# A spectral filter and an MLP on one core: the MLP's second step with weights held and tokens run past

## The chip, the cores and the metric

One core of one Trainium2 chip runs the whole program. The metric is the device time of one execution in microseconds (us). The kernel before took 2520.49 us (median of three runs, 2520.19 to 2525.57). Engines: TensorE (PE, its weight loads PEld), VectorE (DVE), ScalarE (ACT), GpSimd (POOL) and SyncE (SP), which here only issues DMAs.

## What is computed

```python
B, S, D, DFF = 8, 3008, 256, 2048
X = np.fft.rfft(x, axis=1)                       # x: 8 x 3008 x 256
y = np.fft.irfft(X * (filt_r + 1j * filt_i), n=S, axis=1)
t = y.reshape(B * S, D)                          # 24064 tokens
h = t @ w_in                                     # 256 -> 2048
g = h / (1 + np.exp(-1.702 * h))
out = g @ w_out                                  # 2048 -> 256, float32
```

## The kernel before, in words

The sequence length is 64 x 47, so each transform is two matrix steps with a trip through DRAM between them. `fft(b)` does the forward transform, the filter product and the first inverse step of batch b in 46 pieces (`yield`s); `signal(b, t)` does the last inverse step for one tile of tokens and leaves the tile `y` with features on the partitions and tokens along the row, split into a high and a low float32r part. `mlp(b, t, y, nb)` then runs the MLP on a tile of nb blocks of 128 tokens: 4 blocks (512 tokens) in 44 of the 48 tiles, 3 blocks in the last tile of the even batches.

All products of the MLP are done three times, high x high, high x low and low x high, and summed in PSUM. The hidden width is cut into NFC = 16 chunks of 128. `first(fc)` (L592 to L604) does chunk fc of the first step: six matmuls with a 128x128 piece of `wi` held and 512 tokens run past, into a PSUM tile `h`; ACT reads it twice (L601 into `g`, L602 rounded into `gh`) and DVE takes the rest (L603, `gl`). `second(fc)` (L606 to L615) adds chunk fc to the output: for each of the four blocks, the block's `gh` is held and the 512 columns of `wo` (256 high, 256 low) run past (L611), then its `gl` is held and the 256 high columns run past (L615). Each block has a PSUM bank of its own, `pos[i]`, with tokens on partitions. After the last chunk, ACT and DVE add the two halves of each bank into `out` (L625, L626), and SP stores whole rows of 1 KB: two DMAs for a tile (L632), and two of one row per partition (L634) in the four tiles that also carry a row of the neighbouring batch.

PSUM has 8 banks: 2 in the pool `ps_f` (everything of the transforms and of `signal`), 2 in `ps_h` (the chunks `h`), 4 in `ps_o` (`pos`). In the very first transform, `bank` takes tiles from all three pools in turn (L249).

The main loop (L662) goes through the tiles; between the chunks of tile i it lets the next batch's transform take its pieces and, after two of the chunks, the next tile's `signal`. Each engine runs its own instructions in a fixed order; the framework's scheduler chooses that order from an estimated timeline, so it need not be that of the source. The weights arrive as 64-bit floats; `weight` (L184) turns them into float32 and splits them into high (ACT, L209) and low (POOL, L210) parts during tile 0. `wo` lies as [128, chunk, high/low, 256].

Of the kernel before, what the change touches and what calls it, by code (L numbers as in the profile page):

```python
# [9 lines left out]
F32 = mybir.dt.float32  # L10
F32R = mybir.dt.float32r
# [3 lines left out]
ALU = mybir.AluOpType  # L15

B, S, D, DFF = 8, 3008, 256, 2048
N1, N2 = 64, 47
NS = 32
NH = 24  # L20
P = 128
Q = 112
NFC = DFF // P
# [79 lines left out]
def tile_kernel(  # L103
# [12 lines left out]
    nc = tc.nc  # L116
    const = ctx.enter_context(tc.tile_pool(name="const", bufs=1))
    sb = ctx.enter_context(tc.tile_pool(name="sb", bufs=2))
    dram = ctx.enter_context(tc.tile_pool(name="dram", bufs=2, space=bass.MemoryType.DRAM))
    dram1 = ctx.enter_context(tc.tile_pool(name="dram1", bufs=1, space=bass.MemoryType.DRAM))  # L120
    ps_f = ctx.enter_context(tc.tile_pool(name="ps_f", bufs=2, space=bass.MemoryType.PSUM))
    ps_h = ctx.enter_context(tc.tile_pool(name="ps_h", bufs=2, space=bass.MemoryType.PSUM))
    ps_o = ctx.enter_context(tc.tile_pool(name="ps_o", bufs=4, space=bass.MemoryType.PSUM))

    def raw(name):
        return sb.tile([P, 4, D], F32, tag="raw", name=name, bufs=6)
# [16 lines left out]
    HALF = NFC // 2  # L143
    wi_sb, wo_sb = [], []
# [9 lines left out]
    def down(v, q, n=4):  # L154

        return v[:, NH - 1 - q : (NH - 1 - n - q if q + n < NH else None) : -1, :]
# [24 lines left out]
        load_in(w, src)  # L181
        return w

    def weight(w, tu):  # L184

        if w.dtype != F32:
            rv = w.bitcast(U32).rearrange("p a (n k) -> p a n k", k=2)
            low, top = rv[:, :, :, 0], rv[:, :, :, 1]
            t, u = (a.bitcast(U32) for a in tu)
            w = t.bitcast(F32)  # L190


            ins = nc.scalar.activation(t.bitcast(F32), top.bitcast(F32), AF.Abs)
            if first[0]:
                tc.keep_in_program_order(ins)
                first[0] -= 1
            hi, lo = yield
            nc.vector.tensor_scalar(t.bitcast(F32), t.bitcast(F32), LEAST, MOST, ALU.max, ALU.min)
            nc.vector.tensor_scalar(u, t, 3, 0x40000000, ALU.logical_shift_left, ALU.bitwise_xor)
            nc.vector.tensor_scalar(t, u, 0xFF800000, None, ALU.bitwise_and)  # L200
            nc.vector.scalar_tensor_tensor(w, low, 2.0**-52, t.bitcast(F32), ALU.mult, ALU.mult)  # L201
            nc.gpsimd.tensor_tensor(w, u.bitcast(F32), w, ALU.add)
            nc.scalar.activation(w, w, AF.Abs)
            nc.vector.scalar_tensor_tensor(
                w.bitcast(U32), top, 0x80000000, w.bitcast(U32), ALU.bitwise_and, ALU.bitwise_or
            )
        else:
            hi, lo = yield
        nc.scalar.copy(hi, w)  # L209
        nc.gpsimd.tensor_tensor(lo, w, hi.bitcast(F32), ALU.subtract)  # L210
        yield

    def weights():

        todo, tus = [], None
        for i in range(NFC + 4):
            if i < NFC:
                c = slice(P * (i - i % 2), P * (i - i % 2) + 2 * P)
                src = w_out[c, :].rearrange("(c p) d -> p c d", p=P) if i % 2 else w_in[:, c].rearrange("(k p) c -> p k c", p=P)
                todo.append(load_weight(src, f"w_{i}"))  # L220
            if i >= 4:
                if tus is None:
                    tus = const.tile([P, 4, 2, 2, D], F32, tag="zy", name="w_tu")
                for k in range(4 if i == 4 else 1):
                    k = k if i == 4 else i - 1
                    if k < NFC:
                        todo[k] = weight(todo[k], [tus[:, k % 4, m] for m in range(2)])
                        next(todo[k])
                n, o = divmod(i - 4, HALF)
                if n == len(wi_sb):  # L230
                    wi_sb.append(const.tile([P, 2, 2, DFF // 2], F32R, tag=f"wi_{n}", name=f"wi_{n}"))
                    wo_sb.append(const.tile([P, HALF, 2, D], F32R, tag=f"wo_{n}", name=f"wo_{n}"))
                if i % 2:
                    to = [wo_sb[n][:, o - 1 : o + 1, k, :] for k in range(2)]
                else:
                    to = [wi_sb[n][:, k, :, P * o : P * o + 2 * P] for k in range(2)]
                todo[i - 4].send(to)
            yield

    b_of = {}  # L240

    zy = []

# [2 lines left out]
        nc.tensor.matmul(ps, wh, ml, start=False, stop=False)  # L246
        nc.tensor.matmul(ps, wl, mh, start=False, stop=True)  # L247

    banks = [(ps_f, "f"), (ps_o, "o"), (ps_h, "h"), (ps_o, "o")]  # L249
    n_bank = [0]  # L250

    def bank(name):
# [332 lines left out]

    def mlp(b, t, y, nb):

        w = P * nb
        pos = [ps_o.tile([P, 2, D], F32, tag="o", name=f"o_{b}_{t}_{i}") for i in range(nb)]
        gs = {}  # L590

        def first(fc):  # L592
            ps = ps_h.tile([P, 512], F32, tag="h", name=f"h_{b}_{t}_{fc}")
            half, o = divmod(fc, HALF)
            c = slice(P * o, P * o + P)
            for n, (kc, wk, yk) in enumerate([(k, *q) for k in range(2) for q in ((0, 0), (0, 1), (1, 0))]):
                nc.tensor.matmul(ps[:, :w], wi_sb[half][:, wk, kc, c], y[:, yk, kc, :w], start=n == 0, stop=n == 5)  # L597
            g = sb.tile([P, 512], F32, tag="g", name=f"g_{b}_{t}_{fc}")
            gh = sb.tile([P, 512], F32R, tag="gh", name=f"gh_{b}_{t}_{fc}")
            gl = sb.tile([P, 512], F32R, tag="gl", name=f"gl_{b}_{t}_{fc}")  # L600
            nc.scalar.activation(g[:, :w], ps[:, :w], AF.Gelu_apprx_sigmoid)  # L601
            nc.scalar.activation(gh[:, :w], ps[:, :w], AF.Gelu_apprx_sigmoid)  # L602
            nc.vector.tensor_tensor(gl[:, :w], g[:, :w], gh[:, :w].bitcast(F32), ALU.subtract)  # L603
            gs[fc] = gh, gl  # L604

        def second(fc):  # L606
            gh, gl = gs.pop(fc)
            wo = wo_sb[fc // HALF][:, fc % HALF]
            for i in range(nb):
                c = slice(P * i, P * i + P)  # L610
                nc.tensor.matmul(  # L611
                    pos[i].rearrange("p k d -> p (k d)"), gh[:, c],
                    wo.rearrange("p k d -> p (k d)"), start=fc == 0, stop=False,
                )
                nc.tensor.matmul(pos[i][:, 0, :], gl[:, c], wo[:, 0, :], start=False, stop=fc == NFC - 1)  # L615

        first(0)
        for fc in range(NFC):
            if fc + 1 < NFC:
                first(fc + 1)  # L620
            second(fc)
            yield
        o = sb.tile([P, 4, D], F32, tag="out", name=f"out_{b}_{t}")
        for i in range(nb):
            nc.scalar.copy(o[:, i, :], pos[i][:, 1, :])  # L625
            nc.vector.tensor_tensor(o[:, i, :], pos[i][:, 0, :], o[:, i, :], ALU.add)  # L626
        full = 4 if t < 5 else 3
        ov = out.rearrange("(b a n) d -> b a n d", b=B, n=N2)
        for j in range(2):
            n = NH * j + 4 * t  # L630
            dst = ov[b, :, n : n + full, :] if j else down(ov[b], 4 * t)[:, 0:full]
            nc.sync.dma_start(dst, o[64 * j : 64 * j + 64, 0:full, :])  # L632
            if nb > full:
                nc.sync.dma_start(ov[b - 1 + j, :, 0, :], o[64 * j : 64 * j + 64, 3, :])  # L634

    def run(gen, n=None):
        while n is None or n > 0:
# [24 lines left out]
    for i, (b, t) in enumerate(tiles):  # L662
        if t == 0:

            done, chunk, chunks = 0, 0, 6 * NFC - (18 if b == 0 else 8)
            nxt = fft(b + 1) if b + 1 < B else iter(())
        nb = 4 if t < 5 or b % 2 else 3
        sig = start(*tiles[i + 1]) if i + 1 < len(tiles) else iter(())
        for fc, _ in enumerate(mlp(b, t, ys.pop((b, t)), nb)):
            if i == 0:  # L670
                run(w_parts, 1)
                if fc < 5:
                    qs = slice(4 * fc + 4, 4 * fc + 8)
                    load_in(t2_sb[:, qs], t2[:, qs])
                if fc == 12:
                    split_de(de_of[0])
                    tc.keep_in_program_order(nc.vector.memset(f_buf[32:64], 0.0))
                    load_filter()
                    in_order[0] = False
            if i or fc >= 10:  # L680
                chunk += 1
                while chunk <= chunks and done < STEPS * chunk // chunks:
                    run(nxt, 1)
                    done += 1
            if fc in ((11, 13) if t == 5 else (3, 9)):
                run(sig, 1)
        run(sig)
        if i == 0:
            zy.append(const.tile([P, 4, 2, 2, D], F32R, tag="zy", name="zy"))
            nc.gpsimd.memset(zy[0][32:64].bitcast(F32), 0.0)  # L690


_OUTS = [((B * S, D), "float32")]
# [22 lines left out]
```

## Time and profile before

| what | value |
|---|---|
| median of three runs | 2520.49 us |
| profiled execution | 2525.12 us |
| its span, first to last instruction | 2523.3 us |
| granted TensorE clock, mean over the span | 0.987 |
| PE / PEld busy | 96% / 81% |
| DVE / ACT / POOL busy | 62% / 53% / 34% |
| HBM read / written | 158.15 MB / 100.14 MB |

A matmul's record is longer than the slot it takes, since the next one starts while it drains; so the pace of PE is read from the starts of consecutive instructions and not from their durations. In a timeline, consecutive instructions of one kind on an engine are merged into one row with their count. A share of busy time is an average over stages with different limits.

### The profile page before, as it was taken

To read this page: it belongs to the slowest core of one execution; us is meant where nothing else is said; L and a number is where in the kernel's file an instruction comes from. 1 tells how busy PE (TensorE), PEld (TensorE's weight loads), DVE (VectorE), ACT (ScalarE), POOL (GpSimd) and SP (SyncE) were. 2 spreads that over 40 slices of the span, in tenths; PEclk is the share of its full clock that TensorE was granted. 3 is DMA by queue.
4 is the path that set the end of the run, shared out by engine and by line. 5 is a ranking of instruction groups with operands and counts; after the bars stand their busy time and mean duration, and the time that the engine had idled before them with its cause. 6 is when DMAs were issued, how large, how long until landed. Compare 5 with 4: busy or idle time off the path is not lost.

```text
span 2523.3 us, 35230 instructions
## 1 busy us (share of the span) xinstructions
PE 2433.0 (96%) x12540; PEld 2053.8 (81%) x12540; DVE 1556.5 (62%) x2309; ACT 1349.6 (53%) x2546; POOL 847.6 (34%) x734
## 2 busy tenths in 40 slices
PE   5679998999999999999999999999999999999998
PEld 3368887888888888888888888888888888888887
DVE  5784887367763777547773577646775377742222
ACT  4455555555555555555555555555555555644443
POOL 4462443234332444224441344324342244410000
PEclk8789999999999999999999999999999999999999
DMA  8757343453435433453434444355343543330000
GB/s 200 191 153 178 88 97 94 119 126 87 93 92 142 101 92 92 124 132 84 107 80 124 120 102 97 95 130 115 91 100 92 139 95 91 91 71 9 17 9 17
DMA packets 183227, 257.53 MB, mean 102 GB/s; under 512 B 18560, under 2 KB 132910, under 8 KB 183052
## 3 DMA queue, kind: packets, MB, share of 16 engines
q1 hardware_dynamic: 100492, 140.04, 22.0%
q10 hardware_dynamic: 57056, 70.80, 10.5%
q0 software_dynamic: 25504, 44.44, 9.0%
q8 instruction: 100, 1.64, 0.3%
q14 instruction: 75, 0.61, 0.1%
HBM read 158.15 MB, written 100.14 MB: 102 GB/s over the span
## 4 chain that ended last, share of the span: by engine, by line
PE 87%; DMA 5%; DVE 3%; issue 2%; ACT 1%; SPq 0%; POOL 0%; ACTq 0%; DVEq 0%; POOLq 0%
PE h L597 38%; PE o L611 26%; PE o L615 13%; PE i L572 3%; PE s L507 2%; PE i L507 2%; DMA zy<-a_d 1%; DMA br<-b_d 1%; DMA x<-in_x_dram 1%; PE s L245 1%; PE s L247 1%; PE s L246 1%; DVE gl L603 1%; DMA b_d<-b 1%; SPq L135 0%
## 5 line engine op out<-in xcount | busy, mean ns | idle before, releaser
L597 PE MATMUL h<-y,wi 128*128 128x512 f32 (+1 forms) x4608 | 1182.4, 388 | 8.6 <-ACT wi L209 6.8
L603 DVE TENSOR_TENSOR gl<-g,gh 128x512 fp32r<-128x512 f32 (+1 forms) x768 | 627.7, 823 | 738.6 <-ACT gh L602 692.0
L597 PEld LDWEIGHTS h<-y,wi 128*128 128x128 f32 x4608 | 852.7, 189 | 177.3 <-ACT wi L209 7.7
L601 ACT ACTIVATE g<-h 128x512 f32<-128x512 f32 (+1 forms) x768 | 452.7, 590 | 818.4 <-PE h L597 744.2
L611 PE MATMUL o<-wo,gh 128*128 128x512 f32 x3008 | 867.2, 398 | 13.6 <-ACT gh L602 10.1
L611 PEld LDWEIGHTS o<-wo,gh 128*128 128x128 f32 x3008 | 537.4, 189 | 116.2 <-ACT gh L602 12.8
L615 PE MATMUL o<-wo,gl 128*128 128x256 f32 x3008 | 538.3, 283 | 5.9 <-DVE gl L603 5.7
L615 PEld LDWEIGHTS o<-wo,gl 128*128 128x128 f32 x3008 | 477.8, 189 | 64.1 <-DVE gl L603 12.5
L602 ACT ACTIVATE gh<-h 128x512 fp32r<-128x512 f32 (+1 forms) x768 | 446.2, 585 | 72.2 <-PE o L611 62.2
L522 POOL TENSOR_TENSOR zy<-c_buf,zy 48x512 fp32r<-48x512 f32 x224 | 341.8, 1526 | 100.1 <-DVE zy L521 89.3
L441 POOL TENSOR_TENSOR c_buf<-c_buf,u_buf 112x512 f32<-112x512 f32 x128 | 193.2, 1509 | 423.3 <-DVE c_buf L440 423.3
L490 POOL DMA_DIRECT2D zy<-a_d x224 | 128.1, 574 | 383.1 <-PE s L507 114.4
L468 POOL TENSOR_TENSOR xl<-x,xh 128x512 fp32r<-128x512 f32 (+2 forms) x91 | 111.7, 1238 | 427.9 <-ACT xh L467 334.1
L448 DVE TENSOR_TENSOR c_buf<-s,c_buf 48x512 f32<-48x512 f32 x224 | 154.2, 688 | 30.0 <-ACT c_buf L447 24.1
L448 DVE TENSOR_TENSOR b<-i,b 48x512 f32<-48x512 f32 x224 | 154.2, 688 | 13.7 <-ACT b L447 7.5
L447 ACT COPY b<-i 48x512 f32<-48x512 f32 x224 | 130.1, 581 | 44.5 <-PE i L507 35.7
L447 ACT COPY c_buf<-s 48x512 f32<-48x512 f32 x224 | 130.1, 581 | 30.4 <-PE s L507 21.3
L521 DVE CAST zy<-c_buf 48x512 fp32r<-48x512 f32 x224 | 94.1, 420 | 57.5 <-POOL c_buf L441 53.8
L572 PE MATMUL i<-t_sb,br 128*128 128x128 f32 x736 | 102.5, 280 | 14.7 <-DMA br<-b_d 13.5
L572 PEld LDWEIGHTS i<-t_sb,br 128*128 128x128 f32 x736 | 96.3, 196 | 21.1 <-DVE w_tu L201 8.7
L439 DVE TENSOR_TENSOR u_buf<-c_buf,f_buf 48x512 f32<-48x512 f32 x112 | 90.3, 806 | 3.8
L507 PE MATMUL s<-zy,de_sb 112*112 112x512 f32 x210 | 82.9, 406 | 1.1 <-DVE b L448 1.0
(92 smaller groups left out, 1344.1 us busy)
## 6 DMA issues: line engine op xcount, KB each, us to landing
f_buf<-fs SPq DMA_DIRECT2D x224, 192.0 KB
zy<-a_d POOLq DMA_DIRECT2D x224, 192.0 KB, 3.6
b_d<-b ACTq DMA_DIRECT2D x128, 192.0 KB
x<-in_x_dram SPq DMA_DIRECT2D x87, 256.0 KB
a_d<-ah ACTq DMA_DIRECT2D x84, 256.0 KB
a_d<-al ACTq DMA_DIRECT2D x84, 256.0 KB
br<-b_d SPq DMA_DIRECT2D x84, 256.0 KB
out_dram<-out SPq DMA_DIRECT2D x80, 256.0 KB
```

Of the source, the lines that this page charges most:

```text
L441: nc.gpsimd.tensor_tensor(u1, u1, u2, ALU.add)
L447: nc.scalar.copy(dst[h], ps[k][o])
L448: nc.vector.tensor_tensor(dst[h], ps[k][h], dst[h], ALU.add)
L507: nc.tensor.matmul(ps[k][:Q], de_sb[:, k, m], src[:, k], start=True, stop=True)
L522: nc.gpsimd.tensor_tensor(y[o, k], u1[h], y[h, k].bitcast(F32), ALU.subtract)
L572: nc.tensor.matmul(ps[:, P * i : P * i + P], br[m][:, i], t2_sb[:, 4 * t + i, :], start=True, stop=True)
L597: nc.tensor.matmul(ps[:, :w], wi_sb[half][:, wk, kc, c], y[:, yk, kc, :w], start=n == 0, stop=n == 5)
L601: nc.scalar.activation(g[:, :w], ps[:, :w], AF.Gelu_apprx_sigmoid)
L602: nc.scalar.activation(gh[:, :w], ps[:, :w], AF.Gelu_apprx_sigmoid)
L603: nc.vector.tensor_tensor(gl[:, :w], g[:, :w], gh[:, :w].bitcast(F32), ALU.subtract)
L611: nc.tensor.matmul(pos[i].rearrange("p k d -> p (k d)"), gh[:, c], wo.rearrange("p k d -> p (k d)"), start=fc == 0, stop=False,)
L615: nc.tensor.matmul(pos[i][:, 0, :], gl[:, c], wo[:, 0, :], start=False, stop=fc == NFC - 1)
```

## The change

PSUM: `ps_f` gets 4 banks and `ps_o` 2. `wo` is laid out as [128, chunk, high/low, 2, 128]: the 256 output features are dealt into two sets of 128, m = 0 for the even ones and m = 1 for the odd ones (`by_m`), when the weights are split. `second(fc)` holds a 128x128 piece of `wo` and runs `gh` or `gl` past it, 512 tokens at a time, into two PSUM banks `pos[m]` that have features on partitions and tokens along the row. At the end of a tile DVE turns each bank in blocks of 32x32 into `out`, whose partition 32a + x then holds token x of each block of 32 and the 64 features of group a, so that 256 bytes of a token's row lie together. The stores become 16 for a tile (24 in the four tiles with a row of the neighbouring batch), each of 32 partitions and up to 4 pieces of 256 bytes per partition. They go into a list; the next tile's chunks each issue one or two of them on SP, and after the last tile SP and ACT issue them alternately.

```diff
-    ps_f = ctx.enter_context(tc.tile_pool(name="ps_f", bufs=2, space=bass.MemoryType.PSUM))
+    ps_f = ctx.enter_context(tc.tile_pool(name="ps_f", bufs=4, space=bass.MemoryType.PSUM))
-    ps_o = ctx.enter_context(tc.tile_pool(name="ps_o", bufs=4, space=bass.MemoryType.PSUM))
+    ps_o = ctx.enter_context(tc.tile_pool(name="ps_o", bufs=2, space=bass.MemoryType.PSUM))
+    def by_m(a):
+        return a.rearrange("p n (q m) -> p n m q", m=2)
...
+        if order is not None:
+            w = order(w)
         nc.scalar.copy(hi, w)
         nc.gpsimd.tensor_tensor(lo, w, hi.bitcast(F32), ALU.subtract)
...
-                    wo_sb.append(const.tile([P, HALF, 2, D], F32R, tag=f"wo_{n}", name=f"wo_{n}"))
+                    wo_sb.append(const.tile([P, HALF, 2, 2, P], F32R, tag=f"wo_{n}", name=f"wo_{n}"))
...
-    banks = [(ps_f, "f"), (ps_o, "o"), (ps_h, "h"), (ps_o, "o")]
+    banks = [(ps_f, "f"), (ps_o, "o"), (ps_f, "f"), (ps_h, "h")]
...
-        pos = [ps_o.tile([P, 2, D], F32, tag="o", name=f"o_{b}_{t}_{i}") for i in range(nb)]
+        pos = [ps_o.tile([P, 512], F32, tag="o", name=f"o_{b}_{t}_{m}") for m in range(2)]
...
         def second(fc):
-            gh, gl = gs.pop(fc)
+            gp = gs.pop(fc)
             wo = wo_sb[fc // HALF][:, fc % HALF]
-            for i in range(nb):
-                c = slice(P * i, P * i + P)
-                nc.tensor.matmul(
-                    pos[i].rearrange("p k d -> p (k d)"), gh[:, c],
-                    wo.rearrange("p k d -> p (k d)"), start=fc == 0, stop=False,
-                )
-                nc.tensor.matmul(pos[i][:, 0, :], gl[:, c], wo[:, 0, :], start=False, stop=fc == NFC - 1)
+            for n, (wk, gk) in enumerate(((0, 0), (1, 0), (0, 1))):
+                for m in range(2):
+                    nc.tensor.matmul(
+                        pos[m][:, :w], wo[:, wk, m], gp[gk][:, :w],
+                        start=fc == 0 and n == 0, stop=fc == NFC - 1 and n == 2,
+                    )
...
-        o = sb.tile([P, 4, D], F32, tag="out", name=f"out_{b}_{t}")
-        for i in range(nb):
-            nc.scalar.copy(o[:, i, :], pos[i][:, 1, :])
-            nc.vector.tensor_tensor(o[:, i, :], pos[i][:, 0, :], o[:, i, :], ALU.add)
+        o = sb.tile([P, 4, 2, 2, 64], F32, tag="out", name=f"out_{b}_{t}")
+        ov = o.rearrange("p q j h (c m) -> p (q j h) c m", m=2)
+        for m in range(2):
+            nc.vector.transpose(ov[:, : 4 * nb, :, m], pos[m][:, :w].rearrange("p (n c) -> p n c", c=32))
...
+            for h in range(2):
+                for a in range(4):
+                    v, src = rows[b, h, a], o[32 * a : 32 * a + 32, :, j, h, :]
+                    dst = v[:, n : n + full, :] if j else down(v, 4 * t)[:, 0:full]
+                    stores.append((dst, src[:, 0:full]))
+                    if nb > full:
+                        stores.append((rows[b - 1 + j, h, a, :, 0, :], src[:, 3]))
...
         for fc, _ in enumerate(mlp(b, t, ys.pop((b, t)), nb)):
+            for _ in range(-(-len(stores) // (NFC - fc))):
+                store()
...
+    while stores:
+        for queue in (nc.sync, nc.scalar):
+            store(queue)
```

## Rows read from the trace of the kernel before

**Rows 1.** The page: busy time by engine, then the chain that ended last.

```profile
PE 2433.0 (96%) x12540; PEld 2053.8 (81%) x12540; DVE 1556.5 (62%) x2309; ACT 1349.6 (53%) x2546; POOL 847.6 (34%) x734
...
PE 87%; DMA 5%; DVE 3%; issue 2%; ACT 1%; SPq 0%; POOL 0%; ACTq 0%; DVEq 0%; POOLq 0%
```

**Rows 2.** Windows of 50 us: busy us (instructions) by engine, clock, DMA share, GB/s.

```profile
100.00:150.00 50.00, 35.44 (x148) 26.94 (x148) 48.22 (x59) 30.98 (x54) 31.25 (x22) 0.87 0.52 169
...
1500.00:1550.00 50.00, 49.99 (x256) 41.90 (x255) 38.42 (x57) 27.94 (x53) 22.78 (x21) 1.00 0.42 101
...
2300.00:2350.00 50.00, 49.77 (x260) 42.37 (x259) 14.67 (x24) 21.44 (x42) 0.00 (x0) 1.00 0.04 11
```

**Rows 3.** PE's timeline in the last batch: start, us, line, operation, shape, count.

```profile
2306.24 1.53 PE L597 MATMUL h<-y,wi 128*128 128x512 f32 x6
2307.60 0.64 PE L615 MATMUL o<-wo,gl 128*128 128x256 f32 x4
2308.07 1.09 PE L611 MATMUL o<-wo,gh 128*128 128x512 f32 x4
2309.00 1.53 PE L597 MATMUL h<-y,wi 128*128 128x512 f32 x6
```

**Rows 4.** PE's timeline where 512-column matmuls follow one another, in three places.

```profile
494.63 1.54 PE L597 MATMUL h<-y,wi 128*128 128x512 f32 x6
496.01 1.07 PE L611 MATMUL o<-wo,gh 128*128 128x512 f32 x4
496.92 1.52 PE L597 MATMUL h<-y,wi 128*128 128x512 f32 x6
...
2344.53 2.89 PE L597 MATMUL h<-y,wi 128*128 128x512 f32 x12
2347.27 0.64 PE L615 MATMUL o<-wo,gl 128*128 128x256 f32 x4
```

**Rows 5.** Groups by line and shape: count, busy us, mean ns, idle before.

```profile
L601 ACT ACTIVATE g<-h 128x512 f32<-128x512 f32 x704 | 421.0, 599 | 773.3 <-PE h L597 711.6 <-DVE b L448 21.0 <-PE o L615 19.7
L626 DVE TENSOR_TENSOR out<-o,out 128x256 f32<-128x256 f32 x188 | 67.2, 416 | 7.3 <-ACT out L625 6.4
L210 POOL TENSOR_TENSOR wo<-w_tu,wo 128x512 fp32r<-128x512 f32 x8 | 12.1, 1511 | 3.6 <-ACT wo L209 3.5
L367 DVE COPY a_in<-s 128x512 f32<-128x512 f32 x6 | 4.1, 690 | 12.7 <-PE s L365 12.7
```

**Rows 6.** Timeline at a tile's end: PE's last chunk, DVE's sums, PE's next second step.

```profile
1504.27 0.63 PE L615 MATMUL o<-wo,gl 128*128 128x256 f32 x4
1504.97 1.55 PE L597 MATMUL h<-y,wi 128*128 128x512 f32 x6
1506.42 1.42 DVE L626 TENSOR_TENSOR out<-o,out 128x256 f32<-128x256 f32 x4
1507.99 0.39 PE L611 MATMUL o<-wo,gh 128*128 128x512 f32 x1
```

**Rows 7.** PE's own waits: engine line, waited for, us in total, times, longest.

```profile
PE o L611 <- ACT gh L602: 10.1, 11, 4.1
PE o L615 <- DVE gl L603: 5.7, 10, 1.6
PE s L504 <- DMA zy<-a_d: 3.7, 6, 1.8
```

**Rows 8.** DMA issues on SP by line: duration ns min/median/max; then the page's queue row.

```profile
L632 SPq DMA_DIRECT2D out_dram<-out x96: 587/615/1638, 191.2 to 2519.2; - x96
L135 SPq DMA_DIRECT2D f_buf<-fs x224: 302/364/1539, 167.5 to 2193.5; - x112
...
q1 hardware_dynamic: 100492, 140.04, 22.0%
```

**Rows 9.** Timeline of the kernel's end.

```profile
2516.04 0.64 PE L615 MATMUL o<-wo,gl 128*128 128x256 f32 x4
...
2519.82 0.59 SPq L634 DMA_DIRECT2D out_dram<-out  x1
```

More of the change, by code (lines that the diff above doesn't have):

```diff
@@ L182, in load_weight, with weight @@
         return w
-    def weight(w, tu):
+    def by_m(a):
+        return a.rearrange("p n (q m) -> p n m q", m=2)
+    def weight(w, tu, order=None):
         if w.dtype != F32:
@@ L226, in weights @@
                     if k < NFC:
-                        todo[k] = weight(todo[k], [tus[:, k % 4, m] for m in range(2)])
+                        todo[k] = weight(todo[k], [tus[:, k % 4, m] for m in range(2)], by_m if k % 2 else None)
                         next(todo[k])
@@ L231, in weights @@
                     wi_sb.append(const.tile([P, 2, 2, DFF // 2], F32R, tag=f"wi_{n}", name=f"wi_{n}"))
-                    wo_sb.append(const.tile([P, HALF, 2, D], F32R, tag=f"wo_{n}", name=f"wo_{n}"))
+                    wo_sb.append(const.tile([P, HALF, 2, 2, P], F32R, tag=f"wo_{n}", name=f"wo_{n}"))
                 if i % 2:
-                    to = [wo_sb[n][:, o - 1 : o + 1, k, :] for k in range(2)]
+                    to = [wo_sb[n][:, o - 1 : o + 1, k] for k in range(2)]
                 else:
@@ L238, in weights @@
             yield
-    b_of = {}
+    b_of, stores = {}, []
     zy = []
@@ L622, in mlp, with store @@
             yield
-        o = sb.tile([P, 4, D], F32, tag="out", name=f"out_{b}_{t}")
-        for i in range(nb):
-            nc.scalar.copy(o[:, i, :], pos[i][:, 1, :])
-            nc.vector.tensor_tensor(o[:, i, :], pos[i][:, 0, :], o[:, i, :], ALU.add)
+        o = sb.tile([P, 4, 2, 2, 64], F32, tag="out", name=f"out_{b}_{t}")
+        ov = o.rearrange("p q j h (c m) -> p (q j h) c m", m=2)
+        for m in range(2):
+            nc.vector.transpose(ov[:, : 4 * nb, :, m], pos[m][:, :w].rearrange("p (n c) -> p n c", c=32))
         full = 4 if t < 5 else 3
-        ov = out.rearrange("(b a n) d -> b a n d", b=B, n=N2)
+        rows = out.rearrange("(b h r n) (a x) -> b h a r n x", b=B, h=2, n=N2, a=4)
         for j in range(2):
             n = NH * j + 4 * t
[L631 to L634, printed above, removed]
+            for h in range(2):
[5 more added lines that the diff above has]
+                        stores.append((rows[b - 1 + j, h, a, :, 0, :], src[:, 3]))
+    def store(queue=nc.sync):
+        if stores:
+            queue.dma_start(*stores.pop(0))
     def run(gen, n=None):
```

## The prediction

> **What bounds the kernel now.** I read the page first: PE is busy 96% of the span, and the chain that ended last is 87% PE [rows 1]. A share is an average over stages, so the windows come next. In tile 0, while the weights are made, PE is busy 35.4 us of 50 at a granted clock of 0.87; after that it is full, 49.99 us with a transform beside it and 49.77 without, clock 1.00, while DVE has some 12 us or more to spare [rows 2]. From tile 1 on the time is therefore the length of PE's own stream of instructions, and the views to read are the starts in PE's timeline.
>
> One step of the MLP in the last batch runs from 2306.24 to 2309.00, 2.76 us as the rows round it, 2.77 by its parts: the six matmuls of the first step take 2307.60 - 2306.24 = 1.36 us, 0.227 each; the second step takes 0.47 us for four matmuls of 256 columns (0.118 to 0.119 each) and 0.93 us for four of 512 (0.233 each), 1.40 us in all; 6 x 0.227 + 4 x 0.119 + 4 x 0.233 = 2.77 [rows 3].
>
> **The matmuls.** The second step passes the same number of columns before and after: 4 x (512 + 256) = 3072 and 6 x 512 = 3072. What goes are two matmuls and two weight loads per step. So the question is what one of the new six costs. The 256-column ones now cost 0.119, more than half of 0.227. The 512-column ones cost 0.233 where they stand behind 256-column ones [rows 3], but 0.91 / 4 = 0.227 where six matmuls of 512 columns stand before them (496.01 to 496.92) [rows 4]. The twelve first-step matmuls at a tile's start take 2.74 / 12 = 0.228, although the last six write another bank than the first six (2344.53 to 2347.27) [rows 4]. So I take the slower pace to belong to the change of length and not to the line, and price the new six at 0.227 each: 1.36 us. The step becomes 12 x 0.227 = 2.724 us: 0.036 less than 2.76, 0.046 less than 2.77; I take 0.043, nearer to the parts, whose digits are finer.
>
> Steps with 512 tokens: 704 (the count of L601) [rows 5]; 16 of them lie in tile 0, where PE waits for weights, and count for nothing. 688 x 0.043 = 29.6 us. The lower end: each run of shorter matmuls of the transforms is followed by one slower group, as L611 is now, 0.02 us more; some 180 such places (two per tile for the next tile's inverse step, and by the code 12 per batch for seven batches' first step) take back 4 us, so 25. The 64 steps of three-block tiles go from 3 x (0.233 + 0.119) = 1.06 us to six matmuls of 384 columns, halfway between 0.119 and 0.227, 1.04 us: counted as zero.
>
> Here the Trainium skill speaks against the change. *TensorE: Matmul & The Clock Gate*, section "Back-to-back issue gap", gives a warm matmul N/2.4 ns and a fixed 2.5 ns. By it two matmuls fewer at equal columns save 5 ns a step, 3.4 us in all. The rows disagree: by it the 256- and 512-column matmuls would stand 0.109 and 0.216 apart, and they stand 0.119 and 0.227 to 0.233 apart. It is a rival below with a small chance.
>
> **Waits inside a step.** The new order needs `gh` first and `gl` only after four matmuls, 0.9 us later; now the 256-column ones with `gl` come first. PE's waits for `gh` and `gl` are 10.1 and 5.7 us in all [rows 7]. Both chains keep their length (ACT 0.6 us twice, DVE once), so between none and all of the 16 us can go. Only what `gl` is late by, and not what `gh` is, gets easier with certainty; I take 4, most of the 5.7.
>
> **The tile's end.** ACT's and DVE's sums go: 188 of 0.416 us on DVE, 67 us busy [rows 5], beside PE's work now. In come 96 turns of 128x512 out of PSUM. No row shows a turn; the nearest is DVE's copy of the same size out of PSUM, 0.690 us [rows 5], and I take that, so DVE's total stays (66 us). Below that end stands a bare 0.416 us, as for half the columns; above it, twice the copy, 1.38 us. The new cost is not DVE's busy time but that the next tile's second step needs the two banks back. Its cover: at the end shown, the last matmuls of the old tile start at 1504.27, the next tile's twelve first-step matmuls run, and its second step starts at 1507.99; DVE, busy with other things, comes to the sums at 1506.42 and is done at 1507.84 [rows 6]. Two turns of 0.69 from 1506.42 end at 1507.80, in time. So 0, with PE's twelve matmuls (2.74 us) as cover; without it the two turns would cost 1.4 us at each of 47 boundaries. If DVE comes 0.3 us later than here, the bound is 47 x 0.3 = 14 us.
>
> **The stores.** 104 DMAs become 48 x 16 + 4 x 8 = 800. A store of 256 pieces keeps SP for 0.615 us, a load of 192 KB for 0.364 [rows 8]; the new ones have 128 pieces, so I take 0.364 and keep 0.615 as the bound: 6 to 10 us of SP's time per tile of some 49 us, against 1.2 now. They wait for nothing but turns that are over, and their buffer is needed again a tile later. Behind them on SP stand the loads of `x`, `f_buf` and `br`, each late by a store or two. These are asked for a piece or more ahead. PE's own waits for `zy`, fed by such loads, are 3.7 us, at most 1.8 at a time [rows 7]; another 1.8 at each of seven batches would be 13 us, the bound, and I take 0. On the DMA engines, 24064 rows of 1 KB become 96256 pieces of 256 bytes. By the mean of SP's queue, 22.0% x 16 x 2523 / 100492 = 0.088 us a packet [rows 8], the 72192 more would take 16% of the engines' time, and by bytes nothing; they are 42% busy in the middle [rows 2], so there is room at either end.
>
> **The end of the kernel.** The last matmuls start at 2516.04, the last store is issued by 2520.41, the span ends at 2523.3 [rows 9], so a store takes 2.9 us to land. After: about 1.8 us from that start to the last turn, 24 stores over two queues, 12 x 0.364 = 4.4, and 2.9: 9.1 us in place of 7.3, +2 (up to +5 at 0.615 each).
>
> **Tile 0.** `wo` is read with a step of two when it is split, eight times on ACT and on POOL, there 1.51 us each [rows 5]. Between nothing and a doubling of POOL's eight, 12 us; I take 1. Four banks for transforms I cost at nothing: PE never stands still in the windows with a transform [rows 2].
>
> **The sum.** Against the profiled execution (span 2523.3, in all 2525.1): -29.6 - 4 + 2 + 1 = -30.6, so 2494.5. That execution lay 4.6 us over the median of 2520.49, and the median of the changed kernel should be 2490.
>
> **Rivals.**
> The turns hold the banks. Two banks instead of four, each needed within 0.23 us of the other. From 1506.42, two turns of T us must be over by 1508.22, when the second matmul of the next second step would start: the stall is 2T - 1.8. It eats the whole gain at 0.64 us per boundary, T = 1.22 us. With T = 1.38, 0.96 x 47 = 45 us: 2535, slower. For it: no turn is in the trace, and DVE is 77% busy with a transform beside it [rows 2]. Against: the copy's 0.69. Chance 0.10.
> The pace stays. If 0.233 belongs to the second step itself (results going to changing banks, the freshly written `gh`) and not to its neighbours, the step is 6 x 0.227 + 6 x 0.233 = 2.76 us, 0.007 less: 5 us, with the end's 2 about 2518. For it: every group of L611 in the steady step [rows 3]. Against it: L611 at 0.227 behind a long run [rows 4]. Chance 0.07.
> Only columns count. The price of a matmul is its columns, as the page's rule has it: 3 us, with the end's 2 about 2519. For it: equal columns. Against it: 256 columns at 0.119. Chance 0.05.
> All waits in steps go, and the four banks bring the transforms closer together: 12 us more, 2478. For it, the 16 us of rows 7; against it, that the longest of them, 4.1 us, is a single one for `gh`, which is needed no later than now. Chance 0.06.
> The forecast, with 0.72, lies between 2477 (29.6 and all 16 us of waits gained, the end at +2) and about 2512 (25 gained, boundaries or loads at their bound of 14, the start and the end near theirs).
>
> **How the numbers follow.** 0.2%, about 5 us, is what a measurement of this kernel can tell from no change. Faster: the forecast and the last rival, 0.78. Same: pace and columns, 0.12. Slower: the turns, 0.10. The range leaves out the slow case and the two of no change, 2477 to 2512.
>
> **What would show it.** In the last batch's timeline the starts of one step lie 2.72 us apart, and the six matmuls of the new second step 0.227; at 2.76 the pace stayed. A turn's mean duration near 0.69; over 1.2 with PE waiting on it at each tile's start is the slow rival. The second step has 768 x 6 = 4608 matmuls in place of 704 x 8 + 64 x 6 = 6016. SP's issues of 0.36 us with no new waits of PE for `zy` or `br`. I would be wrong above all if the new second step gets a wait of its own once per tile.

## The result

The changed kernel takes 2494.48 us (median of four runs, 2491.34 to 2499.14) against 2520.88 for the kernel before (2520.19 to 2525.57): a ratio of 0.9893, 95% interval 0.9873 to 0.9913, 26 us less. The forecast was 2490, between 2477 and 2512. The profiled execution spans 2492.3 us where that of before spans 2523.3.

The page's first part, the chain's lines and SP's queue row of the changed kernel; they answer to [rows 1, 8]:

```profile
PE 2404.6 (96%) x11132; PEld 1984.6 (80%) x11132; DVE 1559.7 (63%) x2217; ACT 1292.0 (52%) x2358; POOL 838.6 (34%) x734
...
PE o L621 37%; PE h L607 36%; PE i L577 3%; PE i L512 2%; PE s L512 2%; DMA zy<-a_d 1%; SPq L651 1%; DVE gl L613 1%; PE s L250 1%; PE s L251 1%; DMA x<-in_x_dram 1%; PE s L252 1%; SPq L135 1%; DMA br<-b_d 1%; DVE b L453 1%
...
q1 hardware_dynamic: 192268, 139.95, 23.8%
```

PE is still the bound and as full as before; it has 1408 matmuls fewer (12540 - 11132). The chain goes through the second and the first step in near equal shares, and SP's stores (L651) are part of it with 1%. SP's queue moves nearly twice the packets (192268, before 100492) in 23.8% instead of 22.0% of the DMA engines' time, so the added packets cost little there.

PE's timeline in the last batch, which answers to [rows 3]; L607 is the first step, L621 the second:

```profile
2302.67 1.52 PE L607 MATMUL h<-y,wi 128*128 128x512 f32 x6
2304.03 0.62 PE L621 MATMUL o<-gl,wo 128*128 128x512 f32 x2
2304.48 1.07 PE L621 MATMUL o<-gh,wo 128*128 128x512 f32 x4
2305.39 1.52 PE L607 MATMUL h<-y,wi 128*128 128x512 f32 x6
```

A step is 2.72 us (2302.67 to 2305.39); the second half of it 2305.39 - 2304.03 = 1.36 us, 0.227 for each of six matmuls, although they write two banks in turn. The two matmuls with `gl` come first: the scheduler's choice, not the source's.

PE's waits over the whole trace and the groups of the turns and stores, answering to [rows 5, 7, 8]:

```profile
PE o L621 <- ACT gh L612: 12.0, 9, 5.5
PE o L621 <- DVE gl L613: 10.7, 7, 5.2
PE s L509 <- DMA zy<-a_d: 5.2, 6, 1.7
PE i L577 <- DMA br<-b_d: 2.6, 4, 1.1
...
L635 DVE STREAM_TRANSPOSE out<-o 128x512 f32<-128x512 f32 x88 | 58.2, 696 | 19.7 <-PE o L621 19.0
...
L621 PE MATMUL o<-gh,wo 128*128 128x512 f32 x2816 | 782.0, 395 | 13.5 <-ACT gh L612 12.0 <-DVE out L635 1.0 <-POOL wo L215 0.5
...
L651 SPq DMA_DIRECT2D out_dram<-out x816: 315/430/2187, 188.6 to 2489.4; - x164
L651 ACTq DMA_DIRECT2D out_dram<-out x16: 380/432/434, 2482.4 to 2489.4; - x16
```

A turn takes 0.696 us, and PE waited 1.0 us in all for turns. A store takes 0.43 us of its queue, and there are 832.

The kernel's end, answering to [rows 9]:

```profile
2480.64 0.61 PE L621 MATMUL o<-gl,wo 128*128 128x512 f32 x2
2481.06 1.31 DVE L635 STREAM_TRANSPOSE out<-o 128x512 f32<-128x512 f32 x2 [1.14 <-PE o L621]
2482.40 7.40 SPq L651 DMA_DIRECT2D out_dram<-out  x16
2482.41 7.46 ACTq L651 DMA_DIRECT2D out_dram<-out  x16
```

**Where the 31 us of the span came from.** For every matmul of PE I took the time from its start to the start of PE's next one and summed these over the whole trace, from the first `g` of tile 1 on, by what the matmul does. No single row has these sums; waits are in them. The columns add up to the span within 0.3 us. The kernels below the second line are the experiments that follow.

| kernel | until tile 1 | first step | second step | transforms | after PE's last | span |
|---|---|---|---|---|---|---|
| before | 182.9 | 1018.6 | 1056.7 | 258.0 | 6.9 | 2523.3 |
| after | 180.6 | 1011.6 | 1031.3 | 257.2 | 11.4 | 2492.3 |
| a_half | 178.5 | 1018.5 | 1055.1 | 265.4 | 11.3 | 2529.0 |
| a_turn2 | 180.2 | 1022.5 | 1037.4 | 267.1 | 12.6 | 2520.0 |
| a_f2o2 | 176.8 | 1015.7 | 1037.2 | 266.9 | 11.7 | 2508.6 |
| a_f2o4 | 179.1 | 1020.8 | 1038.1 | 273.3 | 11.4 | 2522.8 |
| a_jit | 179.2 | 1022.6 | 1034.2 | 257.8 | 11.4 | 2505.3 |
| a_burst | 180.5 | 1010.0 | 1038.1 | 256.7 | 11.4 | 2496.9 |
| a_pin | 179.9 | 1010.2 | 1032.8 | 259.0 | 11.8 | 2493.9 |
| a_wide | 181.3 | 1013.0 | 1039.1 | 258.3 | 6.6 | 2498.5 |
| a_tail3 | 183.6 | 1010.7 | 1031.7 | 256.7 | 18.2 | 2501.0 |
| b_jit | 177.8 | 1019.6 | 1054.0 | 264.9 | 6.9 | 2523.4 |
| b_gl512 | 181.4 | 1010.4 | 1363.9 | 245.1 | 6.7 | 2807.6 |

From before to after: second step -25.4, first step -7.0, transforms -0.8, until tile 1 -2.3, the end +4.5.

The three middle columns can be split once more, by what a matmul costs and what holds it up. I counted each distance of over 0.3 us as a matmul of 0.227 us and a wait. In the stretches where the granted clock was 0.50 (1.2 GHz) I took twice these lengths and counted half of the time without waits as lost to the clock; that half is an estimate, from 512-column matmuls of the transforms that stand 0.43 us apart there and 0.235 at full clock. No single row has these sums either.

| kernel | matmuls at full clock | waits | lost at clock 0.50 |
|---|---|---|---|
| before | 2294.7 | 36.3 | 2.4 |
| after | 2265.7 | 34.4 | 0.0 |
| a_half | 2295.7 | 43.4 | 0.0 |
| a_turn2 | 2266.2 | 55.9 | 5.0 |
| a_f2o2 | 2262.7 | 50.1 | 7.2 |
| a_f2o4 | 2266.6 | 55.7 | 9.8 |
| a_jit | 2269.2 | 43.8 | 1.7 |
| b_jit | 2293.4 | 38.8 | 6.4 |

The matmuls take 29.0 us less than before. All kernels here with six equal matmuls in a second step lie between 2262 and 2269, the three with eight unequal ones between 2293 and 2296; what the other edits move is waits and clock.

### The profile page after: what moved, and what is told of

It reads as the page before. It is cut to its first block, busy times and chain, and to the rows that moved or that the text cites. A ratio compares the mean times of both kernels' runs of the same rounds, so it can differ in the third digit from the quotient of the medians.

```text
span 2492.3 us, 32886 instructions
## 1 busy us (share of the span) xinstructions
PE 2404.6 (96%) x11132; PEld 1984.6 (80%) x11132; DVE 1559.7 (63%) x2217; ACT 1292.0 (52%) x2358; POOL 838.6 (34%) x734
## 3 DMA queue, kind: packets, MB, share of 16 engines
q1 hardware_dynamic: 192268, 139.95, 23.8%
## 4 chain that ended last, share of the span: by engine, by line
PE 83%; DMA 6%; DVE 5%; issue 2%; SPq 2%; POOL 1%; ACT 1%; ACTq 0%; DVEq 0%; POOLq 0%
PE o L621 37%; PE h L607 36%; PE i L577 3%; PE i L512 2%; PE s L512 2%; DMA zy<-a_d 1%; SPq L651 1%; DVE gl L613 1%; PE s L250 1%; PE s L251 1%; DMA x<-in_x_dram 1%; PE s L252 1%; SPq L135 1%; DMA br<-b_d 1%; DVE b L453 1%
## 5 line engine op out<-in xcount | busy, mean ns | idle before, releaser
L607 PE MATMUL h<-y,wi 128*128 128x512 f32 (+1 forms) x4608 | 1176.4, 387 | 4.0 <-ACT wi L214 2.2
L613 DVE TENSOR_TENSOR gl<-g,gh 128x512 fp32r<-128x512 f32 (+1 forms) x768 | 644.5, 842 | 757.3 <-ACT gh L612 708.8
L607 PEld LDWEIGHTS h<-y,wi 128*128 128x128 f32 x4608 | 862.6, 189 | 177.8 <-ACT wi L214 2.7
L611 ACT ACTIVATE g<-h 128x512 f32<-128x512 f32 (+1 forms) x768 | 452.8, 590 | 967.9 <-PE h L607 826.1
L621 PE MATMUL o<-gh,wo 128*128 128x512 f32 (+1 forms) x3072 | 837.9, 390 | 13.5 <-ACT gh L612 12.0
L621 PEld LDWEIGHTS o<-gh,wo 128*128 128x128 f32 x3072 | 566.1, 189 | 129.8 <-ACT gh L612 16.2
L621 PE MATMUL o<-gl,wo 128*128 128x512 f32 (+1 forms) x1536 | 478.5, 388 | 10.8 <-DVE gl L613 10.7
L621 PEld LDWEIGHTS o<-gl,wo 128*128 128x128 f32 x1536 | 285.0, 188 | 69.5 <-DVE gl L613 15.2
L446 POOL TENSOR_TENSOR c_buf<-c_buf,u_buf 112x512 f32<-112x512 f32 x128 | 187.7, 1467 | 436.6 <-DVE c_buf L445 436.5
L453 DVE TENSOR_TENSOR c_buf<-s,c_buf 48x512 f32<-48x512 f32 x224 | 154.2, 689 | 16.6 <-ACT c_buf L452 10.5
L453 DVE TENSOR_TENSOR b<-i,b 48x512 f32<-48x512 f32 x224 | 154.1, 688 | 7.7 <-ACT b L452 1.4
```

What stands on the lines that cost most here:

```text
L446: nc.gpsimd.tensor_tensor(u1, u1, u2, ALU.add)
L453: nc.vector.tensor_tensor(dst[h], ps[k][h], dst[h], ALU.add)
L621: nc.tensor.matmul(pos[m][:, :w], wo[:, wk, m], gp[gk][:, :w], start=fc == 0 and n == 0, stop=fc == NFC - 1 and n == 2,)
```

## The experiments

Names with a_ are edits of the changed kernel, with b_ of the kernel before. Measured times are medians; ratios are to the kernel before on the same chip.

| kernel | us | ratio, 95% interval |
|---|---|---|
| a_again | 2492.57 | 0.9887 (0.9870 to 0.9903) |
| a_half | 2531.80 | 1.0046 (1.0031 to 1.0061) |
| a_turn2 | 2523.41 | 1.0007 (0.9997 to 1.0016) |
| a_f2o4 | 2523.70 | 1.0011 (1.0001 to 1.0020) |
| a_f2o2 | 2512.63 | 0.9975 (0.9963 to 0.9986) |
| a_jit | 2508.43 | 0.9951 (0.9936 to 0.9966) |
| a_burst | 2499.47 | 0.9918 (0.9901 to 0.9934) |
| a_pin | 2494.70 | 0.9896 (0.9881 to 0.9911) |
| a_wide | 2498.10 | 0.9904 (0.9889 to 0.9919) |
| a_tail3 | 2501.79 | 0.9912 (0.9894 to 0.9931) |
| b_jit | 2526.40 | 1.0016 (1.0006 to 1.0025) |
| b_gl512 | 2809.36 | one run |

**The changed kernel again.**

> The changed kernel once more, on the same chip as the three beside it. 2491 to 2499 us and a ratio to the kernel before of 0.987 to 0.991. One step of the MLP in the last batch 2.72 us, a turn 0.69 us.

2492.57 us: the program itself repeats within a few us. What follows is held against 2492 to 2495.

**Count and length, with the operands as changed.**

> The changed kernel with the last two matmuls of each second step (those with gl) cut into two of 256 columns each: 4 of 512 and 4 of 256 columns, the counts and lengths of the kernel before, but with wo still held and the tokens run past. Theory, the price hangs on count and length: 4 x 0.119 + 4 x 0.233 = 1.41 us in place of 1.36, a step of 2.77 us, and 688 steps give back 30 us: 2524. Rival, the gain comes from who is held (constant weights instead of freshly written gh): the step stays at 2.72 and the time at 2494. Second rival, only columns count: 5 ns a step, 2498.

```diff
-                    nc.tensor.matmul(
-                        pos[m][:, :w], wo[:, wk, m], gp[gk][:, :w],
...
+                    for c in (slice(0, w // 2), slice(w // 2, w)) if n == 2 else (slice(0, w),):
+                        ins = nc.tensor.matmul(
+                            pos[m][:, c], wo[:, wk, m], gp[gk][:, c],
...
+                        if c.start:
+                            tc.keep_in_program_order(ins)
```

The last two lines tie each second half behind its first. PE's timeline in its last batch (L622 is the second step):

```profile
2330.95 1.53 PE L607 MATMUL h<-y,wi 128*128 128x512 f32 x6
2332.32 0.64 PE L622 MATMUL o<-gl,wo 128*128 128x256 f32 x4
2332.79 1.09 PE L622 MATMUL o<-gh,wo 128*128 128x512 f32 x4
2333.72 1.53 PE L607 MATMUL h<-y,wi 128*128 128x512 f32 x6
```

These are the steps of before over again: 0.47 + 0.93 us for the second half, 2.77 in all, with `wo` held and the tokens run past. The time is 2531.8, some 37 us over the changed kernel, 7 more than expected. At full clock its matmuls take 30.0 us more, as worked out; the rest is 9.0 us more of waits, most of them in the transforms, less 2.1 until tile 1. So the gain of the matmuls comes from six equal ones in place of eight unequal ones, and not from who is held; both rivals fall.

**The same from the other side.**

> The kernel before with the matmul of gl run past all 512 columns of wo instead of the 256 high ones (a small product more, the low part times the low part): eight matmuls of 512 columns per second step, blocks of gh and gl held as before. If the pace of 0.233 belongs to the neighbourhood of 256-column matmuls, they now stand 0.227 apart in the last batch: 8 x 0.227 = 1.82 us, a step of 3.18 us, 688 x 0.41 = 285 us more, about 2806 us. If it belongs to holding gh or to the changing banks, 8 x 0.233 = 1.86 us, a step of 3.22 us, about 2840 us.

```diff
-                nc.tensor.matmul(pos[i][:, 0, :], gl[:, c], wo[:, 0, :], start=False, stop=fc == NFC - 1)
+                nc.tensor.matmul(pos[i].rearrange("p k d -> p (k d)"), gl[:, c], wo.rearrange("p k d -> p (k d)"), start=False, stop=fc == NFC - 1)
```

```profile
2604.83 1.52 PE L597 MATMUL h<-y,wi 128*128 128x512 f32 x6
2606.19 1.07 PE L615 MATMUL o<-wo,gl 128*128 128x512 f32 x4
2607.10 1.07 PE L611 MATMUL o<-wo,gh 128*128 128x512 f32 x4
2608.01 1.52 PE L597 MATMUL h<-y,wi 128*128 128x512 f32 x6
```

With `gh` and `gl` held as before and four banks in turn, the same lines now stand 0.91 / 4 = 0.227 apart, a step is 3.18 us, and the time is 2809 where 2806 was worked out. The 0.233 of L611 in the kernel before [rows 3] belonged to its 256-column neighbours, and eight matmuls keep the pace of six as long as they are equal.

**The turns.**

> The changed kernel with each turn done twice, so that a bank is held for 1.38 us instead of 0.69 and the pair for 2.8 us. Slow rival of the prediction: DVE comes to the turns 1.5 us after the last matmul, PE's twelve matmuls cover 2.7 us, so 0.96 us are lost at each of 47 boundaries: 2540. Theory that the cover is longer than that, since the last chunk is turned while the next tile's inverse step and both first steps run, and since the order of the instructions is made anew with the longer turns in view: under 10 us more, 2494 to 2504.

```diff
-        for m in range(2):
+        for m in (0, 0, 1, 1):
             nc.vector.transpose(ov[:, : 4 * nb, :, m], pos[m][:, :w].rearrange("p (n c) -> p n c", c=32))
```

The turns of its trace, and who waited for them:

```profile
L635 DVE STREAM_TRANSPOSE out<-o x192: 540/683/721, 186.7 to 2509.4; 128x512 f32<-128x512 f32 x176, 128x384 f32<-128x384 f32 x16
...
  PE o L621: 6.8, 6
```

2523.4, 29 us over the changed kernel, and neither account fits. PE waits for turns at 6 places, 6.8 us, not at 47 for 45 us; so the cover at most tiles is longer than at the one that the prediction read. Yet the time is not within 10 us either. The matmuls keep their pace; PE's waits of all kinds are 21 us longer, and 5 us are lost where the granted clock was 0.50. How much of the waiting is the longer turns delaying other work of DVE, and how much a worse order, one edit of this kind can't say (see a_jit).

**The banks.**

> The changed kernel with the banks dealt out as before: two for the transforms, four for the outputs, so that the outputs of two tiles have banks at once. Theory: neither matters, since PE waited for no bank in either trace for more than 2 us in all: 2491 to 2499. Rival: the four transform banks carry part of the gain: 5 to 15 us slower, with PE waiting for DVE or ACT at the transform's second matmul. Second rival: the output banks were the tighter ones: 3 to 10 us faster, with no wait of PE for the turns.

```diff
-    ps_f = ctx.enter_context(tc.tile_pool(name="ps_f", bufs=4, space=bass.MemoryType.PSUM))
+    ps_f = ctx.enter_context(tc.tile_pool(name="ps_f", bufs=2, space=bass.MemoryType.PSUM))
-    ps_o = ctx.enter_context(tc.tile_pool(name="ps_o", bufs=2, space=bass.MemoryType.PSUM))
+    ps_o = ctx.enter_context(tc.tile_pool(name="ps_o", bufs=4, space=bass.MemoryType.PSUM))
-    banks = [(ps_f, "f"), (ps_o, "o"), (ps_f, "f"), (ps_h, "h")]
+    banks = [(ps_f, "f"), (ps_o, "o"), (ps_h, "h"), (ps_o, "o")]
```

> The changed kernel with two banks for the transforms, and the two banks that this frees left unused: outputs keep two. With two transform and four output banks the whole gain was gone (2523.7 us). Theory, the transforms need the banks: the same here, 2516 to 2530, with PE waiting for DVE at the transform's matmuls and the transform's matmuls slower than in the changed kernel. Rival, the four output banks did it, by letting the scheduler set the work in another order: 2491 to 2499 here.

```diff
-    ps_f = ctx.enter_context(tc.tile_pool(name="ps_f", bufs=4, space=bass.MemoryType.PSUM))
+    ps_f = ctx.enter_context(tc.tile_pool(name="ps_f", bufs=2, space=bass.MemoryType.PSUM))
```

With the banks of before the whole gain is gone (2523.7); with two transform banks and two unused, two thirds of it (2512.6). In the kernel with two and two: PE's waits from 182 us on, that is from tile 1; two places in its timeline; and a window behind them, first there and then in the changed kernel:

```profile
PE i L577 <- DMA br<-b_d: 9.8, 6, 4.4
PE s L512 <- DVE b L453: 5.9, 11, 1.4
...
PE i L577 <- DVE b L453: 2.2, 1, 2.2
...
PE i L577 <- DVE c_buf L453: 1.1, 1, 1.1
...
337.54 0.49 PE L512 MATMUL s<-zy,de_sb 112*112 112x512 f32 x1 [1.44 <-DVE b L453]
339.16 1.16 PE L577 MATMUL i<-t_sb,br 128*128 128x128 f32 x8 [1.13 <-DVE c_buf L453]
...
340.00:350.00 10.00, 8.13 (x27) 5.70 (x27) 8.59 (x11) 4.58 (x9) 6.73 (x6) 0.66 0.62 134
...
340.00:350.00 10.00, 8.50 (x38) 6.62 (x37) 8.57 (x12) 4.82 (x10) 5.85 (x4) 1.00 0.32 78
```

The matmuls keep their pace at full clock in both kernels. What is lost is waits, 16 and 21 us more than in the changed kernel, and time at the granted clock of 0.50, 7 and 10 us. With two and two, PE waits 9.2 us from tile 1 on for DVE to clear a bank that its next matmul needs (L453; 0.7 in the changed kernel). Twice the clock falls to 0.50 within 3 us of such waits: for 6.8 us after the two shown, and for 3.4 us after the one of 2.2. These fit a want of banks. The waits for `br` grow as well, to 9.8 us from 0.6, and a third fall of the clock stands at one of them. They need not be a want of banks: a_wide, with four, has 8.9 us of them. Nor need all of the rest be one, as the next run shows.

**The order alone.**

> The changed kernel with the next tile's inverse step handed in one chunk later in five of six tiles (after chunks 4 and 10 instead of 3 and 9). No work is added or taken, no bank changed; the scheduler makes another order of it. Theory, the order alone is worth little: 2490 to 2499. Rival, any new order moves the time by 10 us or more, so that the loss with two transform banks and with doubled turns says nothing of banks and turns: under 2485 or over 2505.

> The kernel before with the next tile's inverse step handed in one chunk later, the same edit that made the changed kernel 14 us slower through the order alone. Theory, order is worth up to 15 us in either kernel, in either direction: anything from 2506 to 2536, and its second step keeps 1.40 us. Rival, only the changed kernel with its two output banks is touchy: 2517 to 2525 here.

```diff
-            if fc in ((11, 13) if t == 5 else (3, 9)):
+            if fc in ((11, 13) if t == 5 else (4, 10)):
```

No work and no bank is changed, and the changed kernel takes 2508.4, 14 us more: here the rival, that order counts, is right. The kernel before takes 2526.4, some 4 us more by the ratio of 1.0016: inside the theory's range and 1.4 us over the rival's, so order counts there too, but less. In a_jit the second step loses 3 us, the first 11, the transforms nothing; 9 us of it are waits. So the 18 us of a_f2o2 stand against 14 us that a mere change of order can cost. By the waits for DVE (9.2 against 0.7 us) and half of the 10.2 us of low clock behind them, an estimate, the four banks are worth 8 to 14 us to the changed kernel; the rest is open. The orders tried for the changed kernel's banks and matmuls (the kernel itself, a_pin, a_burst, a_wide, a_jit) give 2494 to 2508, and none is better than its own.

**The stores.**

> The changed kernel with a tile's 16 or 32 stores all issued on SP at the tile's end instead of one or two per chunk of the next. 16 x 0.43 us keep SP for 7 us on end while the loads of the transform stand behind. Theory, the loads have a piece or more of lead and nothing is lost: 2491 to 2499. Rival, the spreading carries part of the gain: 5 to 20 us slower, with more waits of PE for zy and br.

```diff
-            for _ in range(-(-len(stores) // (NFC - fc))):
-                store()
...
+        while stores and i + 1 < len(tiles):
+            store()
         run(sig)
```

2499.5: 5 us over the changed kernel, 0.5 above what was expected, at the lower edge of the rival's range and inside the scatter of orders. PE's waits for `zy` and `br` are 5.1 and 4.6 us (5.2 and 2.6). That is at most 2 us more of the waits that the rival named, so the 5 us are not shown to be the spreading's.

> The changed kernel with its stores as they were before in shape: two DMAs for a tile (four in the tiles with a row of the neighbour), 64 partitions, pieces of 1 KB. The data of out go to wrong places in DRAM; the number of bytes, the turns and the matmuls are the same. Theory, the 256-byte stores cost nothing before the end and 4 to 5 us at the end (16 stores on each of two queues): the end after the last matmul 7 us instead of 11.4, the rest within the scatter of orders, 2480 to 2505. Rival, 72192 more packets hold up the transform's loads: the waits of PE for zy and br, 8 us in the changed kernel, fall under 3, and the time under 2480.

```diff
-            for h in range(2):
-                for a in range(4):
-                    v, src = rows[b, h, a], o[32 * a : 32 * a + 32, :, j, h, :]
...
+            dst = wide[b, :, n : n + full, :] if j else down(wide[b], 4 * t)[:, 0:full]
+            stores.append((dst, flat[64 * j : 64 * j + 64, 0:full, :]))
...
```

The end after PE's last matmul is 6.6 us, as in the kernel before, in place of 11.4: the small stores cost 4.8 us there. Before the end they cost nothing that shows: PE's waits for `zy` and `br` are 4.3 and 12.6 us, not less than the 5.2 and 2.6 with small stores.

> The changed kernel with the last tile's 32 stores issued in turn by SP, ACT and POOL instead of SP and ACT; every instruction before them keeps its place. 11 stores per queue instead of 16, 0.43 us each on SP and ACT and some 0.6 on POOL: 5 to 6.5 us instead of 7.4, the end after the last matmul 9 to 10.5 us instead of 11.4, 2491 to 2496 in all, a difference that only the trace can show. Rival, POOL's stores land later than the others and nothing is gained: the end at 11 us or more.

```diff
-        for queue in (nc.sync, nc.scalar):
+        for queue in (nc.sync, nc.scalar, nc.gpsimd):
```

The end of its timeline; its span is 2501.0:

```profile
2482.62 0.61 PE L621 MATMUL o<-gl,wo 128*128 128x512 f32 x2
2483.05 1.31 DVE L635 STREAM_TRANSPOSE out<-o 128x512 f32<-128x512 f32 x2 [1.14 <-PE o L621]
2484.39 5.27 SPq L651 DMA_DIRECT2D out_dram<-out  x11
2484.39 5.54 ACTq L651 DMA_DIRECT2D out_dram<-out  x11
2484.66 5.30 POOL L651 DMA_DIRECT2D out_dram<-out  x10 [90.98 <-DVE out L635]
```

All is issued in 5.6 us instead of 7.5, but the span ends 11 us after the last issue (2489.96 to 2501.0), where that of the changed kernel ends 2.4 us after it (2489.87 to 2492.3). So nothing is gained, and the end is 18.2 us, as the rival said, but not for its reason. The time from issue to landing of POOL's ten stores, then POOL's drains at the end of the program, here and in the changed kernel:

```profile
DMA to landing us min/median/max: 1.8/2.4/2.9
...
L734 POOLq DRAIN  x3: 40/108/11410, 2488.8 to 2500.8; - x3
...
L734 POOLq DRAIN  x3: 45/102/9979, 2391.2 to 2492.0; - x3
```

POOL's stores have landed by 2492.4. What ends late is the first of the drains with which POOL closes the program: it starts at 2488.8, beside POOL's last stores, and lasts 11.4 us. In the changed kernel the same drain lasts 10.0 us, but it starts at 2391.2, after POOL's last work there, and is over 90 us before the end. One of the four executions took 2493.92 us, 8 us less than the others; it left no trace, and why is open. PE's instructions keep their order, and from tile 1 on PE's sums repeat those of the changed kernel within 1 us a column; so the scatter of a_jit is one of orders, not of executions.

**The order inside a second step.**

> The changed kernel with the six matmuls of a second step tied to the order of the source, so that the two with gl come last; in the changed kernel the scheduler puts them first in most steps, and PE waits 10.7 us in all for gl and 12.0 for gh. Theory, the order gives gl 0.9 us more and most of the 10.7 goes: 2484 to 2490, PE's wait for gl under 4 us. Rival, the wait only moves to gh, which is needed first then: 2491 to 2502, the sum of both waits at 20 us or more.

```diff
-                    nc.tensor.matmul(
+                    ins = nc.tensor.matmul(
...
+                    if n or m:
+                        tc.keep_in_program_order(ins)
```

2494.7, as the changed kernel. PE waits 12.6 us for `gl` and 10.7 for `gh`, 23.3 together, against 10.7 and 12.0. The time and the sum are the rival's; its account is not, since the wait does not move to `gh` but stays with `gl`. From tile 1 on the two together are 6.4 us here and 6.1 in the changed kernel: the wait stays, wherever the two matmuls with `gl` stand.

## Why the prediction was right, step by step

**The matmuls: right.** 0.227 each and a step of 2.72 us, as worked out. Forecast -29.6; at full clock the matmuls take 29.0 us less, 23.4 of it in the second step, 4.3 in the first and 1.2 in the transforms. That a pace can belong to the neighbours was read from a stretch of the kernel before where L611 stood behind six long matmuls [rows 4], and a_half and b_gl512 show it from both sides. The two rivals on the pace, "the pace stays" and "only columns count", fall with the same rows. By the Trainium skill's formula (*TensorE: Matmul & The Clock Gate*, "Back-to-back issue gap"), which that section gives for a matmul by itself, a_half would by estimate have cost 3.4 us; its matmuls cost 30.

**Waits inside a step: wrong.** Forecast -4. Over the whole trace PE's waits for `gh` and `gl` went from 15.8 to 22.7 us. But most of both lies in tile 0, whose steps the prediction counted for nothing. From 182 us on, before and then after:

```profile
PE o L611 <- ACT gh L602: 3.9, 9, 1.4
PE o L615 <- DVE gl L603: 1.4, 5, 0.3
...
PE o L621 <- DVE gl L613: 3.3, 3, 1.6
PE o L621 <- ACT gh L612: 2.8, 4, 1.0
```

From tile 1 on only 5.3 us were there to gain, and `gl` made up 1.4 of them and not 5.7; now they are 6.1. Two steps failed: a total over the trace was read as the price of the steady steps, and "the new order needs `gl` only after four matmuls" does not hold, since the scheduler puts those two first; a_pin shows that the source's order would not have helped. The mistake is some 5 us. The rival that all waits in steps go, with 0.06, falls too.

**The tile's end: right in result.** A turn was put at 0.690 and took 0.696; PE waited for turns 1.0 us in all. The slow rival's price was too high: it took one boundary [rows 6] for 47, and with turns doubled PE waited for them at six places. But that kernel was 29 us slower, mostly by other waits, which I had not priced; a_turn2 can't part the turns from the new order.

**The stores: right before the end, mis-sized at it.** I counted 800 stores; there are 832, since the row of the neighbouring batch is stored in 16 pieces and not in 8, and the last tile has 32 stores and not 24. Each takes 0.43 us and not 0.364. So each queue issues 16 x 0.467 = 7.4 us and not 4.4: the end became 4.5 us longer, not 2, inside the bound of 5. SP's queue got 91776 packets more and not 72192; its share of the DMA engines rose by 1.8 points, near the low end of the 0 to 16 that were allowed.

**Tile 0.** Forecast +1; PE reached tile 1 2.3 us earlier. It does so at anything between 176.8 and 183.6 us in the kernels above, so this is no effect of the change that could be told.

**Four banks for transforms, costed at nothing: right for the kernel before, not for the changed one.** The reasoning was that PE stands still for no bank in the kernel before, and the transforms did take 258.0 us before and 257.2 after. But it holds for the order of work in that kernel alone: in the changed kernel two transform banks cost 18 us (a_f2o2), of which 8.5 are more waits for a bank, up to 5 the lower clock behind them, and the rest may be the order. The term that was missing altogether is the order: the scheduler makes a new one for nearly every edit (a_tail3 kept it), and that alone is worth some 14 us.

**The sum: luck in its small terms.** The span was forecast 30.6 us shorter and came out 31.0 shorter: matmuls -29.0, waits -1.9, clock -2.4, until tile 1 -2.3, the end +4.5. The matmuls carry it, as forecast. The other terms are each off by 2 to 3 us and happen to cancel. The clock stood in no term: in the profiled execution of before it fell to 0.50 for 6.8 us at a wait of 4.5 us for `br`, and in that of after it did not fall from tile 1 until PE's last matmul. The median came out 4.5 us over the forecast of 2490, because 4.6 us were taken off for the profiled execution of before, and that of after lay at its median. It is also a forecast met with an order that none of those tried beats; with that of a_jit it would have been 18 us off, though still inside the range.

## What to carry to other kernels

Where PE is the bound, read the pace from the starts of its matmuls and price an edit by how many there are and how long each is: here eight unequal matmuls of the same columns cost 1.40 us and six equal ones 1.36, and the unequal ones slowed their neighbours too. Read waits by stage before pricing them: here two thirds of the total lay in the first tile. Before believing a difference of half a per cent, make an edit that changes only the order that the scheduler picks, and see how far that alone moves the time. Count the DMAs of the last tile: they stand at the end, uncovered.

## What the runs showed of the hardware

A 512-column matmul of the MLP stands 0.233 us behind its like in the first few after a 256-column one, and 0.227 in a long run of its own length, whatever is held and whichever bank is written ([rows 3, 4], after, a_half, b_gl512). Nearly twice the packets on SP's queue, as the rows of `out` went out in pieces of 256 bytes, raised its share of the DMA engines only from 22.0% to 23.8%. POOL's stores landed 1.8 to 2.9 us after their issue, but POOL's drain at the end of the program lasted 10.0 us in the changed kernel and 11.4 us in a_tail3, where POOL worked up to the end and the program's end waited for it. In a_f2o2 the granted clock fell to 0.50 (1.2 GHz) for 6.8 us after PE had stood 2.6 us within 4 us, and 512-column matmuls of the transforms then stood 0.43 us apart.
